# Dense layer in token order inside the attention steps of a fused attention and expert kernel

## Chip, cores and metric

The kernel runs on one core of a Trainium2 chip, as one program in one launch. The metric is the device time of one execution in microseconds (us); the time before is the median of three runs. A further execution was profiled, and every duration below is from that one execution.

## The reference

```python
# attention: 8 batches, 8 heads, 576 tokens, head dimension 64; causal window of 128, ALiBi slopes
scores = scale * np.matmul(q, k.transpose(0, 1, 3, 2))
...
scores = np.where(mask, scores + bias[None], -1000000000.0)
...
attn_out = np.matmul(attn, v)                       # attn: softmax over the keys
x = attn_out.transpose(0, 2, 1, 3).reshape(B * S, H * D)      # 4608 tokens x 512

# feed-forward: one dense pair of layers, and one of 8 expert pairs for each token
h_dense = np.maximum(x @ w1_dense, 0.0)             # 512 x 512
y_dense = h_dense @ w2_dense
logits = x @ w_gate
expert_idx = np.argmax(logits, axis=1)
probs = ...                                         # softmax of the logits
gate_w = probs[np.arange(N), expert_idx]
for e in range(E):
    mask = expert_idx == e
    h = np.maximum(x[mask] @ w1[e], 0.0)
    y_moe[mask] = gate_w[mask, None] * (h @ w2[e])
return y_dense + y_moe
```

## The kernel before

The program has two stages. The first is attention, in 48 steps: 16 units `u` (a batch and half of its heads, four at a time), and three steps `pr` in a unit (query tiles 0 and 1, tiles 2 and 3, and the last 64 rows). For PE, ACT and DVE the order of the instructions is the order of the calls in the loop `for n in range(NS + 9)`; SyncE (SP) and GpSimd (POOL) are ordered by the framework's scheduler, and each runs its own queue in order. In round `n` the loop calls `scores` for step n (a mask product, then q times k, on PE, then the exponentials on ACT, line 373), `norm` for step n-2 (DVE, line 442, which writes the row-major tile `xrow`), `flip` for step n-3 (four PE transposes, then an ACT copy into `xT`, line 470), `attend` for step n-1 (48 small products of 64 or 65 columns, line 426, into the one buffer `ax`), the turning and rounding of the next unit's q and k, and at last `lo` (DVE, line 392), which splits step n's exponentials into two bf16 parts. `scores` has one pair of PSUM tiles (`sq`), `attend` one (`ax`), and everything else shares two PSUM tiles named `misc`.

When a batch is complete, `gate_a` to `gate_d` compute its logits, the expert of each token and the token's row in `xs_dram`, one region of 4608 rows for each expert. Five indirect DMAs on POOL's queue (line 569) then scatter the batch's rows there: 512 values of x in fp32, the gate weight and the token's number. The 18 weight matrices are loaded by POOL's queue meanwhile (line 79), each one held back by a small POOL copy (`tick`, line 588).

After the last batch DVE computes a table of 43 blocks (lines 673 to 749): which expert, which rows. Then the second stage runs 43 blocks of 128 rows. `fetch(j)` gathers a block's rows by an indirect DMA (line 766), four blocks ahead, into one of five buffers. `turn_x` casts and transposes them (lines 777 to 784). `layer1` loads the block's expert number into a PE register (line 801) and multiplies x by the expert's and by the dense weights (lines 814 and 822: four products of 512 columns each, weights moving, x stationary). ACT applies the rectifier twice, with the gate as a scale for the expert's half (lines 830, 831). `turn_h` transposes both halves (line 791), `layer2` multiplies them by both second matrices into one sum (lines 849 and 857), DVE copies it out (line 865), and an indirect DMA scatters the rows to their tokens (line 866). The order in a block is `turn_h(j)`, `layer1(j+1)`, `turn_x(j+2)`, `layer2(j)`, `fetch(j+4)`.

The expert's weights are addressed with the register: `w_all[:, bass.DynSlice(er, 1), 0, kc, :]` stands as the moving operand (`rhs`) in lines 814 and 857. Each such operand has a register operation of PE's sequencer ahead of the instruction that uses it.

Of the kernel before, what the change touches and what calls it, by code (L numbers as in the profile page):

```python
# [23 lines left out]
def kernel(  # L24
# [12 lines left out]
    nc = tc.nc  # L37
# [18 lines left out]

    NB = NTOK // P + E - 1
    NSLOT = (E - 1) * NTOK + NB * P

    RW = DM + 4  # L60
    GC = DM
    TC = DM + 1
# [5 lines left out]

    xs_dram = dram.tile([NSLOT, RW], I32, name="xs_dram")
    w_all = persist.tile([P, E + 1, 2, 4, FF], BF16, name="w_all")  # L70
    basee = persist.tile([P, E], F32, name="basee")

    def load_weights(i):
# [9 lines left out]

    ph1 = ctx.enter_context(ExitStack())
# [4 lines left out]
    ppool = ph1.enter_context(tc.tile_pool(name="ppool", bufs=6))  # L89
    xpool = ph1.enter_context(tc.tile_pool(name="xpool", bufs=2))  # L90
    gs = ph1.enter_context(tc.tile_pool(name="gs", bufs=2))
# [6 lines left out]
    psum_m = ph1.enter_context(  # L98
        tc.tile_pool(name="psum_m", bufs=2, space=bass.MemoryType.PSUM)
    )  # L100

    kTs, vfs = [], []
    for i in range(2):
        kT = abuf.tile([P, 2, SP_], F32R, name=f"kT{i}")
        nc.gpsimd.memset(kT.bitcast(F32)[:, :, S:SP_], 0.0)
        kTs.append(kT)
        vf = abuf.tile([P, NT, 4, D + 1], F32, name=f"vf{i}")
        nc.gpsimd.memset(vf[TAIL:P, NT - 1, :, :], 0.0)
        nc.gpsimd.memset(vf[:, :, :, D : D + 1], 1.0)
        vfs.append(vf)  # L110
    xrows = []
    for i in range(2):
        xrow = abuf.tile([P, NT, RW], F32, name=f"xrow{i}")
        nc.gpsimd.memset(xrow[:, :, TC + 1 : RW], 0.0)
        xrows.append(xrow)
    lt = abuf.tile([P, SP_], F32, name="ltsb")
# [16 lines left out]
    def load_q(u, eng):  # L133
        b, hq = divmod(u, HQ)
        hs = slice(4 * hq, 4 * hq + 4)
        t = ld.tile([P, R, 2, 32], F32, name="qraw", tag="qraw")
# [10 lines left out]
    def load_v(u):  # L147
        b, hq = divmod(u, HQ)
        hs = slice(4 * hq, 4 * hq + 4)
        vf = vfs[u % 2]  # L150
        for i in range(NT):
            rows = min(P, S - i * P)
            nc.sync.dma_start(
                out=vf[:rows, i, :, 0:D],
                in_=v[b, hs, i * P : i * P + rows, :].rearrange("h p d -> p h d"),
            )
# [7 lines left out]
    def round_qk(u, nm):  # L164
        s = tmp.pop((nm, u))
        if nm == "q":
            d = qtp.tile([P, 2, S], F32R, name="qT", tag="qT")
# [9 lines left out]
    def prep_v(u):  # L177
        vf = vfs[u % 2]
# [23 lines left out]
    sc = [ppool.tile([P, 2, 2 * PW], F32, name="p32", tag="p32") for _ in range(2)]  # L202
# [41 lines left out]
    def more_constants():  # L244
# [39 lines left out]
        nc.vector.tensor_copy(out=jf, in_=jf_i)  # L284

# [14 lines left out]
    jf = consts.tile([P, NB], F32, name="jf")  # L300
    ident_x = {}

    def pool_constants():
# [17 lines left out]
        nc.gpsimd.iota(base_i, pattern=[[NTOK, E]], base=0, channel_multiplier=0)  # L321
# [12 lines left out]
    def scores(u, pr):  # L334
# [36 lines left out]
        for i in range(2):  # L371
            p32 = ppool.tile([P, 2, 2 * PW], F32, name="p32", tag="p32")
# [7 lines left out]
            plo = ppool.tile([P, 2, 2 * PW], BF16, name="plo", tag="plo")  # L380
# [22 lines left out]
    def attend(u, pr):  # L403
# [31 lines left out]
        def norm():  # L435
            if hq == 0 and pr == 0:
                cur[("xrow", b)] = xrows[b % 2]
            xrow = cur[("xrow", b)]
            recip = gs.tile([P, 2, 4], F32, name="recip", tag="recip")
            nc.vector.reciprocal(out=recip[:rows, 0:nt], in_=ax_v[:rows, 0:nt, :, D])  # L440
            xo = xrow[:rows, qis[0] : qis[0] + nt, hq * 256 : hq * 256 + 256]
            nc.vector.tensor_tensor(  # L442
                out=xo.rearrange("p t (h d) -> p t h d", h=4),
# [3 lines left out]
            )  # L447

        return norm

    def flip(u, pr):
# [4 lines left out]
        if hq == 0 and pr == 0:  # L456
            cur[("xT", b)] = xpool.tile([P, 4, S], F32, name="xT", tag="xT", bufs=1)
        xT = cur[("xT", b)]
        xrow = cur[("xrow", b)]
        tp = psum_m.tile([P, 2, 2, P], F32, name="tp", tag="misc")  # L460
        for i in range(nt):
            for c in range(2):
                c0 = hq * 256 + c * P
                nc.tensor.transpose(
                    out=tp[:, i, c, 0:rows],
                    in_=xrow[:rows, qis[i], c0 : c0 + P],
# [3 lines left out]
        nc.scalar.copy(  # L470
            out=xT[:, 2 * hq : 2 * hq + 2, q0 : q0 + nt * rows].rearrange(
                "p c (t x) -> p t c x", t=nt
            ),
            in_=tp[:, 0:nt, :, 0:rows],
        )

    scat_group = "scatters"
    gst = {}

    def gate_a(b):  # L480
        xT = cur[("xT", b)]
        HF = S // 2
        for hf in range(2):
            lp = psum_m.tile([P, 512], F32, name="lp", tag="misc")
            for ds in range(4):
                nc.tensor.matmul(  # L486
                    out=lp[32 * ds : 32 * ds + 32, 0:HF],
                    lhsT=wg_pad[:, ds, :],
                    rhs=xT[:, ds, hf * HF : (hf + 1) * HF],
# [3 lines left out]
            nc.scalar.copy(out=lt[:, hf * HF : (hf + 1) * HF], in_=lp[:, 0:HF])  # L493
# [50 lines left out]
    def gate_d(b):  # L544
# [11 lines left out]
        slot = gs.tile([P, NT], I32, name="slot", tag="slot")  # L556
# [10 lines left out]
        for t in range(NT):  # L567
# [6 lines left out]
            )  # L574
            tc.declare_no_dep(
                ins.ins,
                group=scat_group,
                reason="every token has a row of its own",
            )
            tc.add_to_no_dep_group(scat_group, ins.ins)  # L580

    def tick(u, pr, i):
# [3 lines left out]
        xrow = cur[("xrow", u // HQ)]  # L586
        c0 = (u % HQ) * 256
        nc.gpsimd.tensor_copy(  # L588
            out=w_all[:TAIL, e, wi, 0, 0:1], in_=xrow[:TAIL, KP[pr][0], c0 : c0 + 1]
# [3 lines left out]
    NS = len(steps)  # L593
    with tc.manual_schedule(engines={ENG.PE, ENG.Activation, ENG.DVE}):
# [7 lines left out]
        norms, later = {}, {}  # L602
        wnext = 0
        for n in range(NS + 9):
            for f in later.pop(n, []):
# [7 lines left out]
            if 0 <= n - 3 < NS:  # L613
                flip(*steps[n - 3])
                u2, pr2 = steps[n - 3]
                if u2 % HQ == HQ - 1 and pr2 == 2:
                    for i, f in enumerate((gate_a, gate_b, gate_c, gate_d)):
                        later.setdefault(n + 1 + i, []).append(
                            lambda f=f, b=u2 // HQ: f(b)
                        )  # L620
            if n == 0:
                more_constants()
                prep_v(0)
            if 0 <= n - 1 < NS:
                norms[n - 1] = attend(*steps[n - 1])
            if n < NS:
                if pr == 0:
                    if u + 1 < NU:
                        load_v(u + 1)
# [3 lines left out]
                elif pr == 1:  # L633
                    if u + 1 < NU:
                        round_qk(u + 1, "k")
                        turn(u + 1, "q")
                        if u + 2 < NU:
                            load_q(u + 2, nc.sync)
                else:
                    if u + 1 < NU:  # L640
# [4 lines left out]
            if 6 <= n < NS and n % 2 == 0 and wnext < 18:  # L645
                tick(*steps[n - 2], wnext)
                load_weights(wnext)
                wnext += 1
        assert wnext == 18

    ph1.close()

    with ExitStack() as ph2:
        rt = ph2.enter_context(tc.tile_pool(name="route", bufs=1))
        mpool = ph2.enter_context(tc.tile_pool(name="mpool", bufs=3))
        NXR = 5
        xrs = []
        for i in range(NXR):
            xr = rt.tile([P, RW], F32, name=f"xr{i}")
            nc.gpsimd.memset(xr, 0.0)  # L660
            xrs.append(xr)
        psum_t = ph2.enter_context(
            tc.tile_pool(name="psum_t", bufs=1, space=bass.MemoryType.PSUM)
        )
        psum_h = ph2.enter_context(
            tc.tile_pool(name="psum_h", bufs=2, space=bass.MemoryType.PSUM)
        )
        psum_y = ph2.enter_context(
            tc.tile_pool(name="psum_y", bufs=2, space=bass.MemoryType.PSUM)
        )  # L670

        n8 = rt.tile([P, E], F32, name="n8")
        nc.vector.tensor_tensor(out=n8, in0=basee, in1=base0, op=ALU.subtract)
        nb_i = rt.tile([P, E], I32, name="nb_i")
# [245 lines left out]
```

## Time and profile before

| | |
|---|---|
| median of 3 runs | 511.72 us (509.45 to 516.21) |
| profiled execution, device time | 514.72 us |
| its span, first to last instruction | 513.0 us |
| mean granted PE clock | 0.882 |
| busy: PE, DVE, ACT, POOL | 383.8, 304.0, 200.3, 172.5 us |
| last product of `attend` ends | 268.7 us |
| first product of `layer1` starts | 304.1 us |
| last product of `layer2` ends | 503.0 us |

The four last rows cut the span into attention (268.7 us), the wait for the last batch's routing (35.4), the blocks (198.9) and the end (10.0), which add up to 513.0. "PE busy" is a union of modelled instruction spans; a product of 512 columns is shown 379 ns long although the next one starts 216 ns later, so a busy share of PE overstates its load.

### The profile page before, as it was taken

How to read it: one execution, taken by the hardware profiler on the slowest of the kernel's cores; microseconds unless marked ns; L12 is line 12 of the kernel's file. 1: busy time of each engine (PE TensorE's matmuls, PEld its weight loads, DVE VectorE, ACT ScalarE, POOL GpSimd, SP SyncE). 2: the span in 40 equal slices, each digit the busy share in tenths (PEclk: the TensorE clock that was granted, in tenths of full speed). 3: DMA queues.
4: the chain of work that ended last, by engine and by line, in shares of the span. 5: the costliest groups of instructions: out<-in, count | busy, mean ns of one | idle time of the engine just before them, and what ended most of it. 6: DMA issues, size and time to landing. Idle time of an engine off the chain costs nothing.

```text
span 513.0 us, 10730 instructions
## 1 busy us (share of the span) xinstructions
PE 383.8 (75%) x4143; PEld 240.0 (47%) x4180; DVE 304.0 (59%) x567; ACT 200.3 (39%) x287; POOL 172.5 (34%) x244
## 2 busy tenths in 40 slices
PE   1567877778776787777783039899998999889891
PEld 0345555555554556555562015444454444445450
DVE  5879797775977669867471514444444444444441
ACT  2527656626567156671541003323333222322230
POOL 2000016042151321613113433445545455535531
PEclk9999878876799768997696559999999999999997
DMA  4644979879698697986102220323323333323210
GB/s 135 178 115 118 201 156 246 186 187 210 153 251 175 186 209 166 255 159 202 45 24 90 74 82 33 115 91 98 102 86 111 101 124 103 114 83 119 80 52 0
DMA packets 70912, 66.92 MB, mean 130 GB/s; under 512 B 42446, under 2 KB 61902, under 8 KB 70864
## 3 DMA queue, kind: packets, MB, share of 16 engines
q0 software_dynamic: 19328, 37.91, 29.5%
q1 hardware_dynamic: 51140, 28.01, 20.1%
q8 instruction: 34, 0.56, 0.4%
q10 hardware_dynamic: 396, 0.33, 0.2%
q14 instruction: 14, 0.11, 0.1%
HBM read 58.56 MB, written 20.78 MB: 155 GB/s over the span
## 4 chain that ended last, share of the span: by engine, by line
PE 24%; DMA 13%; DVE 5%; issue 3%; ACT 3%; POOL 1%; another core or an unknown queue 1%; POOLq 0%; DVEq 0%
DMA xr<-xs_dram,row_i 13%; PE y L849 4%; PE y L857 4%; PE hd L822 4%; PE hm L814 4%; ACT hr L831 2%; PE hps L791 2%; DVE xm L777 2%; PE xps L780 2%; PE ax L426 1%; PE lp L486 1%; POOL xs_dram L569 1%; PE lg L498 1%; DMA xs_dram<-xrow,slot 1%
## 5 line engine op out<-in xcount | busy, mean ns | idle before, releaser
L426 PE MATMUL ax<-vf,p 128*128 128x65 bf16 (+1 forms) x576 | 74.9, 215 | 50.6 <-DVE xrow L442 44.5
L373 ACT ACTIVATE p<-sq 128x1024 f32<-128x1024 f32 (+1 forms) x96 | 69.3, 776 | 92.5 <-PE sq L363 70.8
L392 DVE TENSOR_TENSOR plo<-p 128x1024 bf16<-128x1024 f32 (+1 forms) x96 | 82.6, 900 | 28.6 <-ACT p L373 23.1
L426 PEld LDWEIGHTS <-p 128*128 128x128 bf16 (+1 forms) x1152 | 69.9, 113 | 61.2 <-DVE xrow L442 51.2
L830 ACT ACTIVATE hr<-hm,xr 128x512 bf16<-128x512 f32 x43 | 29.5, 687 | 159.7 <-PE hm L814 159.7
L426 PE MATMUL ax<-vf,plo 128*128 128x65 bf16 (+1 forms) x576 | 74.3, 212 | 3.9 <-DVE plo L392 2.8
L866 POOL DMA_INDIRECT out_dram<-yo,tok_i x43 | 44.5, 1034 | 97.1 <-DVE hT L797 88.5
L426 PE MATMUL ax<-vl,p 128*128 128x64 bf16 (+1 forms) x576 | 74.4, 211 | 0.3 <-issue 0.3
L569 POOL DMA_INDIRECT xs_dram<-xrow,slot x40 | 42.7, 1067 | 87.2 <-DVE xrow L561 44.9
L426 PEld LDWEIGHTS <-plo 128*128 128x128 bf16 (+1 forms) x576 | 63.1, 113 | 3.4 <-DVE plo L392 3.3
L865 DVE COPY yo<-y 128x512 f32<-128x512 f32 x43 | 29.7, 692 | 58.0 <-PE y L857 54.1
L352 PE MATMUL sq<-mask,ident_b 128*128 128x512 bf16 (+1 forms) x177 | 46.9, 370 | 15.0 <-DVE mask L235 9.2
L766 POOL DMA_INDIRECT xr<-xs_dram,row_i x43 | 43.8, 1019 | 19.9 <-ACT hr L831 11.3
L822 PE MATMUL hd<-w_all,xT 128*128 128x512 bf16 x172 | 45.0, 385 | 0.0
L849 PE MATMUL y<-w_all,hT 128*128 128x512 bf16 x172 | 44.2, 379 | 0.9 <-DVE hT L797 0.9
L780 PE MATMUL xps<-ident_b,xm 128*128 128x128 bf16 x172 | 17.3, 225 | 36.4 <-DVE xm L777 35.8
L857 PE MATMUL y<-w_all,hT 128*128 x172 | 44.1, 379 | 0.0
L814 PE MATMUL hm<-w_all,xT 128*128 x150 | 40.7, 388 | 3.8 <-DMA xr<-xs_dram,row_i 2.7
L363 PE MATMUL sq<-qT,kT 32*128 32x256 f32 (+2 forms) x640 | 34.7, 330 | 3.4 <-ACT qT L168 3.4
L588 POOL CAST w_all<-xrow 64x1 bf16<-64x1 f32 x18 | 8.1, 447 | 85.4 <-DVE xrow L442 85.1
L784 DVE COPY xT<-xps 128x512 bf16<-128x512 bf16 x43 | 18.3, 425 | 31.0 <-PE xps L780 31.0
L363 PEld LDWEIGHTS sq<-qT,kT 32*128 32x128 f32 x640 | 26.3, 217 | 21.9 <-issue 14.4
(115 smaller groups left out, 570.2 us busy)
## 6 DMA issues: line engine op xcount, KB each, us to landing
kraw<-in_k_dram SPq DMA_DIRECT2D x16, 576.0 KB
vf<-in_v_dram SPq DMA_DIRECT2D x64, 128.0 KB
w_all<-in_moe_w_dram POOLq DMA_DIRECT2D x16, 512.0 KB
qraw<-in_q_dram SPq DMA_DIRECT2D x62, 128.0 KB
vf<-in_v_dram SPq DMA_DIRECT2D x16, 64.0 KB
w_all<-in_moe_w_dense_dram POOLq DMA_DIRECT2D x2, 512.0 KB
qraw<-in_q_dram SPq DMA_DIRECT2D x15, 64.0 KB
xr<-xs_dram,row_i POOLq DMA_INDIRECT x43, 3.4
```

The source lines that it names most:

```text
L352: nc.tensor.matmul(out=sq[g // 2][:, g % 2, 0:tot], lhsT=ident_b, rhs=rhs, start=True, stop=False,)
L363: nc.tensor.matmul(out=sq[g // 2][:, g % 2, i * wid : i * wid + nq], lhsT=kT[32 * g : 32 * g + 32, c, kj * P : kj * P + P], rhs=qT[32 * g ...
L373: nc.scalar.activation(out=p32[:, :, 0:tot], in_=sq[i][:, :, 0:tot], func=ACT.Exp, scale=SCALE,)
L392: nc.vector.tensor_tensor(out=plo[:, :, 0:tot], in0=p32[:, :, 0:tot], in1=phi[:, :, 0:tot], op=ALU.subtract,)
L426: nc.tensor.matmul(out=ax[:rows, i, o0 : o0 + w], lhsT=lhs, rhs=rhs, start=(n == 1), stop=(n == 3 * len(kl)),)
L569: ins = nc.gpsimd.indirect_dma_start(out=xs_dram[:, :], out_offset=bass.IndirectOffsetOnAxis(ap=slot[:rows, t : t + 1], axis=0), in_=xrow. ...
L766: nc.gpsimd.indirect_dma_start(out=xm_i.bitcast(I32)[:, :], out_offset=None, in_=xs_dram[:, :], in_offset=bass.IndirectOffsetOnAxis(ap=row ...
L814: nc.tensor.matmul(out=hm, lhsT=xT[:, kc, :], rhs=w_all[:, bass.DynSlice(er, 1), 0, kc, :], start=(kc == 0), stop=(kc == 3),)
L822: nc.tensor.matmul(out=hd, lhsT=xT[:, kc, :], rhs=w_all[:, E, 0, kc, :], start=(kc == 0), stop=(kc == 3),)
L849: nc.tensor.matmul(out=y, lhsT=hT[:, c, :], rhs=w_all[:, E, 1, c, :], start=(c == 0), stop=False,)
L857: nc.tensor.matmul(out=y, lhsT=hT[:, 4 + c, :], rhs=w_all[:, bass.DynSlice(er, 1), 1, c, :], start=False, stop=(c == 3),)
L866: nc.gpsimd.indirect_dma_start(out=out[:, :], out_offset=bass.IndirectOffsetOnAxis(ap=tok_i[:, 0:1], axis=0), in_=yo[:, :], in_offset=None ...
```

## The change

The dense pair of layers leaves the blocks. It is computed in token order, batch by batch, inside the attention steps (`dense1`, `dense2`, from a bf16 copy `xTb` of the transposed x, with eight products of 512 x 288 and five of 128 x 512 a batch), and its fp32 result is scattered by five more indirect DMAs a batch to `ys_dram`, at the same rows as x. x itself is scattered in bf16. A block fetches both rows by two plain DMAs on SP's queue, addressed by a register, does the expert alone, and adds the dense row when it leaves PSUM.

The expert's first layer now has the weights as the stationary operand, so that its result comes out transposed and `turn_h` goes. The first 16 blocks are taken from whole blocks that the first six batches fill, so that their table is computed during attention; the rest are routed after the last batch. Rows behind an expert's last one are filled by 16 DMAs (`fill_x`, `fill_y`) with a token number out of range. The two stages become one loop, and the last batches' gates and dense products run between the first blocks. Three v buffers instead of two; v is loaded a unit earlier; the weights are loaded from the first round on, the first three without a hold.

```diff
@@ norm: x in fp32 for the transposes, and a cast of it into xrow
+            xf = xpool.tile([P, 2, 256], F32, name="xf", tag="xf")
-            xo = xrow[:rows, qis[0] : qis[0] + nt, hq * 256 : hq * 256 + 256]
...
+            nc.vector.tensor_copy(
+                out=xrow[:rows, qis[0] : qis[0] + nt, hq * 256 : hq * 256 + 256],
+                in_=xf[:rows, 0:nt],
+            )
@@ flip: two copies out of PSUM instead of one
+        for dst in (cur["xT"], cur[("xTb", b)][:, 2 * hq : 2 * hq + 2, :]):
+            nc.scalar.copy(
+                out=dst[:, :, q0 : q0 + nt * rows].rearrange(
...
@@ gate_a: for each unit, on half the rows of lt, instead of for each batch
@@ new
+    def dense1(b, c, hf):
...
+        hp = psum_m.tile([P, 512], F32, name="hp", tag="misc")
+        for kc in range(4):
+            nc.tensor.matmul(
+                out=hp[:, 0:HF],
+                lhsT=w_all[:, E, 0, kc, c * P : c * P + P],
+                rhs=xTb[:, kc, hf * HF : hf * HF + HF],
+                start=(kc == 0),
+                stop=(kc == 3),
+            )
+        nc.scalar.activation(
+            out=hT[:, c, hf * HF : hf * HF + HF], in_=hp[:, 0:HF], func=ACT.Relu
+        )
+
+    def dense2(b, t):
...
+        yp = psum_m.tile([P, 512], F32, name="yp", tag="misc")
+        for c in range(4):
+            nc.tensor.matmul(
+                out=yp[:rows, :],
+                lhsT=hT[:, c, t * P : t * P + rows],
+                rhs=w_all[:, E, 1, c, :],
...
+        yt = xpool.tile([P, DM], F32, name="yt", tag="yt")
+        nc.scalar.copy(out=yt[:rows, :], in_=yp[:rows, :])
+        ins = nc.gpsimd.indirect_dma_start(
+            out=ys_dram[:, :],
...
+    def dense_items(b):
+        one = [lambda c=c, h=h: dense1(b, c, h) for h in range(2) for c in range(4)]
+        two = [lambda t=t: dense2(b, t) for t in range(NT)]
+        return [one[0:2], one[2:4], one[4:6], one[6:8], two[0:2], two[2:5]]
@@ routing in two tables
+    def route_late():
...
+        for e in range(E):
+            r = nc.values_load(
+                base_r[0:1, e : e + 1],
+                engines=[ENG.SP],
...
+            ins = nc.sync.dma_start(
+                out=xs_dram[bass.DynSlice(r, P), :], in_=fill_x.bitcast(I32)[:, :]
+            )
...
@@ a block
+    def fetch(j):
+        r = nc.values_load(where[j][1], engines=[ENG.SP], ...
+        xr = mpool.tile([P, RW], F32, name="xr", tag="xr", bufs=4)
+        yr = mpool.tile([P, DM], F32, name="yr", tag="yr", bufs=4)
+        for nm, t, src in (("x", xr, xs_dram), ("y", yr, ys_dram)):
+            ins = nc.sync.dma_start(
+                out=t.bitcast(I32)[:, :], in_=src[bass.DynSlice(r, P), :]
+            )
...
     def layer1(j):
...
+        hp = psum_h.tile([P, 4, P], F32, name="hpm", tag="hpm")
+        for c in range(4):
+            for kc in range(4):
+                nc.tensor.matmul(
+                    out=hp[:, c, :],
+                    lhsT=w_all[:, bass.DynSlice(er, 1), 0, kc, c * P : c * P + P],
+                    rhs=xT[:, kc, :],
+                    start=(kc == 0),
+                    stop=(kc == 3),
+                )
+        hT = mpool.tile([P, 4, P], BF16, name="hTm", tag="hTm")
+        nc.scalar.activation(out=hT, in_=hp, func=ACT.Relu)
...
     def layer2(j):
...
+                rhs=w_all[:, bass.DynSlice(er, 1), 1, c, :],
...
+        nc.vector.scalar_tensor_tensor(
+            out=yo,
+            in0=y,
+            scalar=xr[:, GC : GC + 1],
+            in1=yr,
+            op0=ALU.mult,
+            op1=ALU.add,
+        )
+        ins = nc.gpsimd.indirect_dma_start(
+            out=out[:, :],
...
+    AHEAD = 3
+
+    def block(j):
...
+        if j + 1 < NB:
+            layer1(j + 1)
+        if j + 2 < NB:
+            turn_x(j + 2)
+        layer2(j)
+        if j + AHEAD + 1 < NB:
+            fetch(j + AHEAD + 1)
@@ the loop
+        while jm < NB:
...
+            todo = items.pop(n, [])
+            for f in todo[:1]:
+                f()
             if 0 <= n - 1 < NS:
                 norms[n - 1] = attend(*steps[n - 1])
+            for f in todo[1:]:
+                f()
...
+            while wnext < 2 * (E + 1) and n < NS and wnext <= 2 + 16 * (n - 3) / 42:
+                if n > 4:
+                    pace(wnext)
                 load_weights(wnext)
                 wnext += 1
+            if n == NS + 1:
+                ph1.close()
...
+                for j in range(AHEAD + 1):
+                    fetch(j)
+            if n > NS + 1:
+                block(jm)
+                jm += 1
```

Seen in the program that results: each of `layer1`'s 16 products has a register operation ahead of its weight load and another ahead of the product itself, 32 in a block, and `layer2`'s four products have one each; before, a block had eight in all. The scatter of block j, which reads the token numbers in `xr`, has to land before `fetch(j+4)` may write that buffer. ACT's third copy into `yt` in a batch waits for the first scatter out of `yt` to land, the fourth for the second, the fifth for the third.

## The prediction

> **What bounds the kernel now.** I read the busy shares by stage first, because the mean over the span mixes stages. Columns: PE, PEld, DVE, ACT, POOL busy (instructions), granted clock, DMA share, GB/s.
>
> ```profile
> 60.00:260.00 200.00, 155.11 (x2297) 112.14 (x2303) 148.07 (x250) 110.46 (x155) 57.00 (x68) 0.81 0.78 183
> 268.70:304.00 35.30, 5.73 (x42) 3.95 (x44) 11.12 (x42) 1.69 (x5) 14.95 (x20) 0.55 0.28 91
> 304.00:503.00 199.00, 182.87 (x1178) 94.80 (x1198) 90.62 (x168) 55.22 (x86) 91.30 (x122) 0.99 0.29 91
> ```
>
> In attention no engine is full: of 200 us PE works 155 and DVE 148, at a granted clock of 0.81. The 35.3 us behind it hold little but scatters and tables. In the blocks PE works 183 of 199 us at full clock. The list of waits between 60 and 260 us says what attention's engines wait for (total, times, longest).
>
> ```profile
> PEld L426 <- DVE xrow L442: 38.2, 24, 5.6
> PE ax L426 <- DVE xrow L442: 33.0, 18, 5.5
> DVE plo L392 <- ACT p L373: 20.9, 10, 4.3
> DVE vl L181 <- DMA vf<-in_v_dram: 9.4, 6, 2.5
> DVE qs L161 <- DMA qraw<-in_q_dram: 6.8, 3, 3.2
> ```
>
> It is a ring: `attend` waits for DVE to empty `ax`, DVE for ACT's exponentials, ACT for PE's scores. Units start 16.1 us apart (exponentials of step pr=0 at 62.73 in u3, 256.49 in u15); PE idles 3.5 of these, DVE works 11.9, ACT 8.9.
>
> For the blocks I took the chain that ended last, one stretch of it (start, length, what).
>
> ```profile
> 393.34 3.37 DMA xr<-xs_dram,row_i
> ...
> 397.70 0.86 PE y L849 x4
> 398.56 0.86 PE y L857 x4
> 399.43 0.45 PE hps L791 x8
> 399.88 0.86 PE hm L814 x4
> 400.74 0.88 PE hd L822 x4
> 401.62 0.02 issue
> 401.64 0.61 ACT hr L831
> 402.25 0.19 issue
> 402.44 3.33 DMA xr<-xs_dram,row_i
> ```
>
> A block is 3.9 us of PE work, and a loop through the fetch closes over two blocks: 402.44 − 393.34 = 9.1, or 4.55 each; 43 blocks take 198.9, or 4.63 each. PE's array and the transfer loop stand side by side, so relieving one alone brings little. The last view is PE's sequencer, which reads registers (ns min/median/max; first and last start).
>
> ```profile
> L857 PEldq FUSED_REGOPS  x172: 55/55/55, 310.2 to 501.5; - x172
> L801 PEldq TENSOR_LOAD <-er_i x43: 297/328/570, 303.0 to 494.6; - x43
> ```
>
> A register operation lasts 55 ns, but consecutive ones start 133 apart (median of 258 gaps between the four of a layer). So register operation, weight load with a fixed address and product with a register address together occupy the sequencer 133 ns. Fixed pairs go at up to 31 ns each (`attend`: 48 pairs in 1.5 us). A product with a register address therefore costs between 133−55−31 = 47 and 133−55 = 78 ns of sequencer time. I take 62, between them. In before this is hidden: eight in a block are 1.1 us of 4.6.
>
> **The change, part by part**, against the profiled execution (span 513.0 = attention 268.7 + gap 35.4 + blocks 198.9 + end 10.0; 1.7 more outside it).
>
> *Gap.* Sixteen blocks are routed from six batches, so the first blocks need no last gate. Between the last `attend` and the first block remain the scores' tail, PSUM changing hands, a fetch (landings 2.0 to 3.4) and a transpose: 4 us instead of 35.4, bounds 2 and 10. The second table (`route_late`, DVE, near block 7) and the last batch's ten scatters move in between the blocks. The first table, 7.3 us of DVE (the old one ran 288.0 to 295.9) and 2.2 more, moves into steps 43 and 44; DVE is in attention's ring, so I count 4.
>
> *Block, sequencer.* `layer1` issues 16 weight loads and 16 products, all addressed by the register: 32 register operations, where before had four there. A pair costs 2 × (55 + 62) = 234 ns; with 47 and 78 it is 204 and 266; if a load with a register address were as cheap as a fixed one, 188. Sum: register load to first register operation 0.51 (0.40 to 0.67 in before) + 16 × 0.234 = 3.74 + `layer2` 4 × 0.133 = 0.53 + four transposes 0.12 = 4.90 us. Bounds 4.06 (by 188), 4.3 and 5.5.
>
> *Block, the rest.* Array work shrinks to 16 × 0.056 + 0.86 + 0.22 = 2.0 us, hidden under the sequencer. DVE does 0.43 + 0.69, ACT 0.6, POOL one indirect DMA of 1.0: all beside. Gone are the dense half and `turn_h`, 2.2 us of PE's array. The transfer loop: `fetch(j+4)` waits for the scatter of block j; `layer2` 1.05, `yo` 0.69, 0.8 to the issue, scatter 2.1, two DMAs on SP 2.0 to 3.4, 0.3 to the cast: 7.1 to 8.3 over two blocks, 3.55 to 4.2 each. The fetch leaves POOL's queue (1.0 us of POOL each) for SP's, where only the next fetches, and once the fills, stand behind its wait; who waits for them is `turn_x` on DVE two blocks later. The loop stays under 4.9; if the sequencer were quick, this would be the floor. So 43 × 4.90 = 210.7 instead of 198.9.
>
> *Extras among the blocks.* SP's queue holds 16 fills (395 KB a pair, 3.2 MB; attention's `kraw`, 576 KB, lands in 3.8 us) between fetch(10) and fetch(11). POOL issues ten scatters about 1.3 us apart ahead of some blocks' `out`. With four blocks fetched ahead most is hidden: 5 + 4 = 9, bounds 0 and 25 (3.2 MB at `kraw`'s rate is 21, plus 4).
>
> *Attention.* A unit gets half a batch's dense work. PE: 16 × 0.121 (288 of 512 columns, 0.215 at full length) + 10 × 0.215 = 4.1 us at full clock. ACT: a second copy of `flip` 1.47, four rectifiers 1.6, 2.5 copies of `yt` 1.5, in all 5.0 with half a gate copy. DVE: the cast into `xrow`, 1.1. ACT goes from 8.9 to 13.9, DVE from 11.9 to 13.0, both below 16.1. On PE, 12.5 + 4.1 = 16.6 at most, 14.3 if the longer busy stretches bring the clock to 1.00. The cover is PE's idle time behind `xrow`, 3.5 a unit at most; the ring's order is fixed, the dense products stand ahead of and behind `attend`, and both `misc` tiles are shared, so I let two thirds (2.4) fit and charge 1.7 × 16 = 27. With full cover it is 0, without any 4.1 × 16 = 66. Also, ACT's third, fourth and fifth `yt` copies wait for scatters of 5.3 us; behind them ACT has `qT` and the next exponentials, and PE's scores wait for those. Against it, v is loaded a unit earlier and the 9.4 us of waits for it may go, the bound below nothing. With 4 for the table, attention's surplus is 31, bounds −9 and 70. Three unheld weight loads at the start: 0 to 4, taken 0.
>
> *Sum.* 268.7 + 31 + 4 + 210.7 + 9 + 10 = 533.4 span, 535.1 device time, 20.4 above its 514.7. Against the median, 3.0 lower: 532.
>
> **A rule against the row.** The trace's row is the 133 ns spacing, which is longer than a product of 128 columns takes in the array (56). The Trainium skill, "TensorE: Matmul & The Clock Gate", section "Back-to-back issue gap", gives about 81 ns for each sustained pair of weight load and 128-column matmul, as a rule of array and weight loads alone. By it `layer1` would be an estimated 16 × 0.081 = 1.3 us, the block would fall to its transfer loop of 4.2, and the sum to about 502. The same page, "Step-by-step: what each phase is for", puts a matmul decoded in microcode at about 62 ns, which speaks for the sequencer as a bound. The row decides; attention's 31 ns pairs already differ from the 81.
>
> **Rivals.**
> - *The sequencer keeps up* (faster). Loads with a register address overlap more than products do, as the 31 ns pairs suggest, and the block falls to 3.7, inside the transfer loop's 3.55 to 4.2: 43 × 1.2 = 52 less, 480. Against it: nothing in before shows such a load. It decides below 4.19 us a block, where the whole is 2% under the median.
> - *Attention swallows the dense work* (within 2%). PE's idle 3.5 a unit takes all of it and the clock rises; the surplus is the table's 4: 532 − 27 = 505. For it: a first unit undisturbed took 11.7 us. Against it: two `misc` tiles and a fixed order.
> - *The yt and xf buffers stall the ring* (slower, above the forecast). Scatters of 5.3 us behind two `yt` tiles hold ACT, and the single qT tile makes that PE's wait: all 4.1 us show, surplus 70, 571. It decides once ACT's wait passes PE's idle 3.5 a unit.
> - *The early start fails* (slower). If the first fetch waits for all scatters, not those of six batches, the gap stays near 25 instead of 4: 553. The diff's manual dependencies name six batches, which speaks against it.
>
> **How the numbers follow.** Forecast 0.50, its own range 512 to 552 (attention's surplus 15 to 45, block 4.7 to 5.1); sequencer 0.16; swallowed 0.20; stall 0.09; no early start 0.05. The likeliest is 532. For 8 in 10 the range goes from 500, which takes in most of the 505 case and leaves out the 480 one, to 562, short of the 571 case. About 2%, 501.5 to 522, is what a measurement of this kernel can tell from no change. Faster has the sequencer case and the low edge of the swallowed one, 0.17; within 2% the rest of that and the forecast's low end, 0.21; slower the remainder, 0.62.
>
> **What would show it.** In the changed profile: PE sequencer gaps of about 117 ns between register operations in `layer1` and blocks 4.9 apart (wrong if 4.2 or less); units of some 17.8 us with waits of ACT for `ys_dram` and of PE for `misc`; first block within 10 us of the last `attend`; no pause over 10 us near block 10. A surplus of attention under 10 us, or blocks under 4.2, makes the forecast wrong; both in full would give 532 − 27 − 52 = 453.

## The result, and the profile after

The changed kernel takes 668.71 us (median of four runs, 665.05 to 672.0). Before takes 513.97 beside it; the ratio is 1.302 (95% interval 1.289 to 1.316). The forecast was 532 with a range of 500 to 562: the direction is right, the size is not, 20 us forecast and 155 measured.

The same cut of the span, in us (the profiled executions):

| | before | forecast | after |
|---|---|---|---|
| attention, to the last product of `attend` | 268.7 | 268.7 + 31 | 416.9 |
| gap to the first product of `layer1` | 35.4 | 4 | 10.4 |
| 43 blocks | 198.9 | 210.7 + 9 | 232.5 |
| end | 10.0 | 10 | 9.5 |

The busy shares by stage, with the columns of the first view before:

```profile
60.00:260.00 200.00, 145.99 (x1706) 95.22 (x1720) 110.19 (x194) 101.48 (x175) 47.56 (x56) 0.80 0.52 130
416.90:427.20 10.30, 6.65 (x33) 3.16 (x34) 1.30 (x4) 4.12 (x9) 2.90 (x3) 0.99 0.68 209
506.00:659.70 153.70, 146.85 (x761) 74.20 (x771) 38.37 (x65) 19.11 (x32) 31.27 (x32) 0.83 0.41 127
```

In the 200 us in the middle of attention every engine does less than before, ACT included: 101 us instead of 110, although each unit gives it more to do. So the ring is slower because its members wait longer, not because one of them is full. The waits in the same stretch (total, times, longest):

```profile
ACT yt L666 <- DMA ys_dram<-yt,slot: 21.7, 9, 4.7
ACT hTd L649 <- remote: 20.0, 3, 7.1
DVE recip L462 <- remote: 15.0, 2, 7.5
PEld lp L513 <- ACT yt L666: 14.8, 6, 4.7
```

Units are now 26.0 us apart (exponentials of step pr=0 at 110.1 in u4, 370.2 in u14) instead of 16.0 (78.0 and 238.0). A batch, two units, shows two holes. The first, on the chain that ended last (start, length, what): ACT may not write the third `yt` before the scatter of the first has landed, then the same with the next, and PE's `lp` stands behind ACT.

```profile
222.11 6.37 DMA ys_dram<-yt,slot
...
228.57 0.59 ACT yt L666
...
229.43 3.79 DMA ys_dram<-yt,slot
...
233.32 0.59 ACT yt L666
233.91 0.04 issue
233.95 1.18 PE lp L513 x4
```

The second hole comes with the five scatters of x. In the window DVE has 0 instructions and ACT 0.01 us in 7 us; in the timeline (start, length, engine, line, what, idle time before) ACT waits 7.07 us for PE's products of `dense1`, which PE's own rows show over at 205.1. It goes on at 209.08, after POOL has issued its fifth scatter at 206.97:

```profile
202.00:209.00 7.00, 3.96 (x48) 2.61 (x45) 0.00 (x0) 0.01 (x1) 4.66 (x5) 0.74 0.59 176
```

```profile
203.15 0.97 POOL L599 DMA_INDIRECT xs_dram<-xrow,slot  x1 [0.30 <-issue]
204.00 1.15 PE L642 MATMUL hp<-xTb,w_all 128*128 128x288 bf16 x4
...
206.97 0.91 POOL L599 DMA_INDIRECT xs_dram<-xrow,slot  x1 [0.30 <-issue]
209.02 0.21 DVE L462 RECIPROCAL recip<-ax 128x8 f32<-128x8 f32 x1 [7.46 <-remote]
209.08 0.41 ACT L649 ACTIVATE hTd<-hp 128x288 bf16<-128x288 f32 x1 [7.07 <-remote]
```

"Remote" means that the profile found no releaser. Engines tell each other of finished work by semaphores, and the trace has the times of these signals. Set against PE's modelled ends, most of PE's signals arrive within 0.02 us, but here they come late, the one above by 3.9 us (205.15 to 209.08), and there is a like group in each batch. I call these late completions.

In the blocks the sequencer sets the pace, as forecast: 1376 register operations, 32 a block, and each pair in `layer1` starts 0.23 us after the one before (median 227 ns between products). A steady block takes 4.76 us.

```profile
L881 PEldq FUSED_REGOPS  x1376: 3/55/724, 426.0 to 657.5; - x197
```

```profile
440.18 0.22 PE hpm L881
440.41 0.22 PE hpm L881
440.64 0.22 PE hpm L881
```

### The profile page after: what moved, and what is told of

Its sections match the earlier page's. It is cut to its first block, busy times and chain, and to the rows that moved or that the text cites. A ratio compares the mean times of both kernels' runs of the same rounds, so it can differ in the third digit from the quotient of the medians.

```text
span 669.2 us, 12798 instructions
## 1 busy us (share of the span) xinstructions
PE 492.8 (74%) x4378; PEld 287.9 (43%) x4424; DVE 286.2 (43%) x567; ACT 241.3 (36%) x412; POOL 148.2 (22%) x193
## 4 chain that ended last, share of the span: by engine, by line
issue 32%; PE 20%; DMA 18%; ACT 8%; POOL 8%; DVE 7%; another core or an unknown queue 3%; SPq 2%; POOLq 1%; ACTq 0%; DVEq 0%
DMA ys_dram<-yt,slot 11%; POOL out_dram L913 5%; PE hpm L881 4%; DMA qraw<-in_q_dram 4%; PE sq L373 3%; ACT p L394 3%; POOL xs_dram L599 3%; PE hp L642 3%; DVE plo L413 2%; PE sq L384 2%; PE lp L513 2%; DMA vf<-in_v_dram 2%; PE y L897 1%; ACT yt L666 1%
## 5 line engine op out<-in xcount | busy, mean ns | idle before, releaser
L881 PE MATMUL hpm<-xTm,w_all 128*128 128x128 bf16 x688 | 137.2, 240 | 12.0 <-DVE xTm L866 4.2
L881 PEld LDWEIGHTS <-w_all 128*128 x688 | 68.9, 106 | 91.9 <-issue 33.3
L913 POOL DMA_INDIRECT out_dram<-yo,xr x43 | 42.1, 979 | 173.8 <-DVE yo L905 159.0
L642 PE MATMUL hp<-xTb,w_all 128*128 128x288 bf16 x256 | 48.1, 317 | 34.1 <-ACT xTb L497 32.6
L667 POOL DMA_INDIRECT ys_dram<-yt,slot x40 | 41.6, 1040 | 112.1 <-ACT yt L666 107.4
L513 PE MATMUL lp<-xT,wg_pad 128*32 128x288 f32 x128 | 31.0, 585 | 45.4 <-ACT yt L666 21.8
L447 PEld LDWEIGHTS <-plo 128*128 128x128 bf16 (+1 forms) x576 | 61.9, 111 | 4.4 <-DVE plo L413 4.4
L897 PE MATMUL y<-w_all,hTm 128*128 x154 | 58.2, 502 | 1.9 <-issue 1.1
L658 PE MATMUL yp<-w_all,hTd 128*128 128x512 bf16 (+1 forms) x147 | 43.6, 408 | 19.6 <-ACT yt L666 13.1
L649 ACT ACTIVATE hTd<-hp 128x288 bf16<-128x288 f32 x64 | 27.2, 425 | 72.0 <-remote 44.9
L905 DVE SCALAR_TENSOR_TENSOR yo<-y,xr,yr 128x512 f32<-128x512 f32 x43 | 32.3, 750 | 38.5 <-PE y L897 36.0
```

The source lines that it names most:

```text
L447: nc.tensor.matmul(out=ax[:rows, i, o0 : o0 + w], lhsT=lhs, rhs=rhs, start=(n == 1), stop=(n == 3 * len(kl)),)
L513: nc.tensor.matmul(out=lp[r0 : r0 + 32, 0:HF], lhsT=wg_pad[:, 2 * (u % HQ) + c, :], rhs=cur["xT"][:, c, hf * HF : (hf + 1) * HF], start=Tr ...
L642: nc.tensor.matmul(out=hp[:, 0:HF], lhsT=w_all[:, E, 0, kc, c * P : c * P + P], rhs=xTb[:, kc, hf * HF : hf * HF + HF], start=(kc == 0), s ...
L658: nc.tensor.matmul(out=yp[:rows, :], lhsT=hT[:, c, t * P : t * P + rows], rhs=w_all[:, E, 1, c, :], start=(c == 0), stop=(c == 3),)
L667: ins = nc.gpsimd.indirect_dma_start(out=ys_dram[:, :], out_offset=bass.IndirectOffsetOnAxis(ap=slots[b][:rows, t : t + 1], axis=0), in_=y ...
L881: nc.tensor.matmul(out=hp[:, c, :], lhsT=w_all[:, bass.DynSlice(er, 1), 0, kc, c * P : c * P + P], rhs=xT[:, kc, :], start=(kc == 0), stop ...
```

## The experiments

All times in us. The times of after and of e7 to e10 are medians of several executions, the others are one execution each; the first columns cut the profiled span as above. The groups of runs stood on different chips: before, run beside them, took 516.2 (e1 to e4), 513.8 (e5 to e8), 505.6 (e9 to e12), 518.5 (e13 to e15) and 518.8 (e16 to e18). And two executions differ: e6's attention is 8.1 shorter than after's, though its edit lies in the blocks alone. Differences of attention of a few us are therefore not read as effects below.

| run | attention | gap | blocks | end | time |
|---|---|---|---|---|---|
| after | 416.9 | 10.4 | 232.5 | 9.5 | 668.7 |
| e1 dense2 in three steps | 388.6 | 6.5 | 231.2 | 9.5 | 637.6 |
| e2 scatters of x in five steps | 383.2 | 10.8 | 235.0 | 9.3 | 640.1 |
| e3 both | 357.4 | 5.7 | 232.1 | 9.7 | 606.7 |
| e4 no dense work | 293.6 | 5.6 | 218.3 | 6.1 | 525.4 |
| e5 as e3, scatters in three steps | 362.0 | 5.8 | 232.3 | 9.6 | 611.5 |
| e6 fixed expert | 408.8 | 10.4 | 187.5 | 9.5 | 618.2 |
| e7 before, scatters in three steps | 269.0 | 35.1 | 197.6 | 10.1 | 514.7 |
| e8 dense in the blocks, early routing | 292.5 | 5.9 | 184.2 | 6.1 | 489.4 |
| e9 as e8, q loaded once | 281.4 | 4.1 | 179.3 | 6.1 | 471.1 |
| e10 as e9, weights held | 275.2 | 4.0 | 179.3 | 6.1 | 465.6 |
| e11 as e3, quarter of the products | 355.2 | 4.6 | 229.5 | 9.7 | 600.8 |
| e12 as e3, q once, weights held | 341.5 | 5.7 | 229.1 | 9.3 | 587.3 |
| e13 as e3, flip first | 356.8 | 5.7 | 231.2 | 9.7 | 605.2 |
| e14 as e3, dense copies on DVE | 428.3 | 9.4 | 234.6 | 9.3 | 683.3 |
| e15 as e12, flip first | 345.0 | 5.7 | 234.7 | 9.3 | 596.5 |
| e16 as e13, quarter of the products | 355.5 | 4.9 | 231.7 | 9.7 | 603.6 |
| e17 as e3, no scatter of y | 338.7 | 5.7 | 229.4 | 6.1 | 581.6 |
| e18 as e16, no scatter of y | 332.1 | 4.7 | 228.0 | 6.5 | 572.9 |

**The two holes.**

```diff
@@ e1: dense_items, by step
-        return [one[0:2], one[2:4], one[4:6], one[6:8], two[0:2], two[2:5]]
+        return [[], one[0:3], one[3:6], one[6:8], two[0:2], two[2:3], two[3:5]]
@@ e2: gate_d issues the first scatter of x, each later step one more
+        scatter_x(b, xrow, 0)
+        for t in range(1, NT):
+            gates.setdefault(gst["n"] + t, []).append(
+                lambda b=b, xrow=xrow, t=t: scatter_x(b, xrow, t)
+            )
...
+        nc.vector.tensor_copy(out=sc_t, in_=slots[b][:, t : t + 1])
```

> The five second-layer items of a batch stand in three steps (2, 1, 2) instead of two (2, 3), and the first layer in steps two to four, so that the scatter out of each yt buffer has a step of its own to land before ACT writes that buffer again. Theory yt (ACT's wait for its two yt buffers, 45 us between 100 and 400 us, sets attention's surplus): attention 45 us shorter, 625 us in all. Theory burst (PE's completions arrive 3 to 5 us late while POOL issues five scatters of x back to back, and ACT and DVE stand still for 7 us a batch): within 10 us of 669. Theory work (the ring has no room for 8 us of PE and 10 us of ACT a batch): within 10 us of 669, the wait only changes its name.

> The five scatters of x of a batch are issued one in each of five steps (each behind a small copy of its slot column on DVE) instead of back to back. Theory burst: the 7 us in which ACT and DVE stand still in each batch go to 1 or 2, 40 us less, 630 us. Theory yt and theory work: within 10 us of 669.

> Both spreads together. If both causes are real and separate: 85 us less, 585 us. If the work itself sets the surplus: still over 640 us.

Attention falls by 28.3 (e1), 33.6 (e2) and 59.4 (e3): both holes are real, and they nearly add (61.9). 45 and 40 were expected, and e3's time lies between its two cases. In e1 ACT's wait for landings of y falls from 45.1 to 16.4 within attention, so that what went off the list is what was gained; its edit also regroups the first layer's items. In e2 the "remote" waits of ACT and DVE are gone, and a new wait has come, of DVE's cast into `xrow` for the scatters that are now spread out (38.8). What ACT now waits for is PE's products as such, 1.1 us at a time:

```profile
ACT hTd L657 <- PE hp L650: 21.3, 20, 3.2
```

Late completions of over 1 us stand in five groups between 60 and 360 us in after, one to a batch (around 105, 158, 208, 259 and 313 us); in e2 no such group is left. So the burst of scatters makes the groups. What in the chip delays the signal is not shown.

**Without dense work, and the row tile.**

```diff
@@ e4: fetch_in no longer fetches yr, the last copy of a block adds none, and the loop
-                    for i, fs in enumerate(dense_items(b2)):
-                        items.setdefault(n + 1 + i, []).extend(fs)
@@ e5: as e3, two scatters in the first step, and
-            gates.setdefault(gst["n"] + t, [])
+            gates.setdefault(gst["n"] + t // 2, [])
```

> The dense products, their scatters and the fetches of the dense rows are left out (the output lacks the dense half); the blocks and the early routing stay. All theories: attention near that of before, 275 to 290 us, and 530 to 545 us in all. What it tells: if the 7 us stand-still of each x burst is still there without dense items, the burst alone makes it (attention nearer 300); if it is gone, it needs a dense item behind it.

> As the kernel with both spreads, but the five scatters of x stand in three steps (2, 2, 1) instead of five, so that the last has landed before the row tile is written for the next batch but one; there DVE's cast into it waited 47 us between 100 and 350 us for these scatters. Theory late rows: attention 15 to 25 us shorter than 357, 580 to 592 us in all. Theory work (what is left of attention's surplus over the kernel without dense items, 64 us, is PE's and ACT's work on them): within 8 us of 607.

e4 puts dense work at 416.9 − 293.6 = 123.3 us of attention, and 14 us of the blocks. Its units are 16.1 us apart, as in before, with the bursts back to back, and "remote" waits of ACT and DVE come to 2.2 us between 60 and 420 (67.4 in after): without a dense item in the ring the bursts cost nothing that shows. Its attention still ends 24.9 later than in before, and 20.9 of this stand at the start (u4 begins at 98.9 instead of 78.0). In e5 DVE's wait for late rows, 46.8 us in e3, is gone, but attention is not shorter: ACT's wait for landings of y grows from 13.1 to 19.7 between 100 and 350 us, and DVE's for ACT's exponentials from 24.5 to 51.2. Taken away alone, the late rows are worth nothing.

**The block's sequencer.**

```diff
@@ e6: layer1 and layer2
-                    lhsT=w_all[:, bass.DynSlice(er, 1), 0, kc, c * P : c * P + P],
+                    lhsT=w_all[:, 0, 0, kc, c * P : c * P + P],
...
-                rhs=w_all[:, bass.DynSlice(er, 1), 1, c, :],
+                rhs=w_all[:, 0, 1, c, :],
```

> The changed kernel with expert 0's weights at fixed addresses in both layers of a block: no register operations, everything else the same (the output is that of expert 0 for all rows). Theory sequencer (32 register operations of 113 ns make the block's 4.76 us): blocks fall to the transfer loop, 3.6 to 4.2 us, 620 to 645 us in all. Rival (the transfer loop or a chain over ACT and DVE already sets the block): 4.6 us or more, over 660 us.

The steady block falls from 4.76 to 4.08 (24 blocks between the `out` scatters at 503.2 and 601.0), and the stage by 45.0. In equal stretches PE's busy time, which was full, drops to 60%; the first line is after, the second e6:

```profile
550.00:600.00 50.00, 47.85 (x248) 24.46 (x251) 12.23 (x21) 5.97 (x10) 10.75 (x11) 0.80 0.41 126
```

```profile
550.00:600.00 50.00, 29.58 (x297) 20.58 (x294) 14.44 (x26) 7.45 (x13) 11.74 (x12) 0.93 0.50 156
```

That is the sequencer. At 4.08 the transfer loop (3.55 to 4.2 in the prediction) takes over: between 503 and 600 us PE's first transposes of a block wait 41.1 us for landings of `xr`, where they waited 5.2 in after. The total, 618.2, lies just under its forecast of 620 to 645; attention, which the edit doesn't touch, was 8.1 shorter.

**Before, and the early routing alone.** e7 gives before the scatters of e5. e8 computes the dense layers in the blocks again, as before does, with x stationary and the weights moving in the expert's first product, rows fetched five blocks ahead, and keeps the routing from six batches; no `yr` is written or fetched.

```diff
@@ e8: layer1, first the expert's product, then the dense one; turn_h then transposes hr
+                lhsT=xT[:, kc, :],
+                rhs=w_all[:, bass.DynSlice(er, 1), 0, kc, :],
...
+                    lhsT=w_all[:, E, 0, kc, c * P : c * P + P],
+                    rhs=xT[:, kc, :],
@@ e9
-        load_q(2, nc.sync)
@@ e10
-            while wnext < 2 * (E + 1) and n < NS and wnext <= 2 + 16 * (n - 3) / 42:
+            if 6 <= n < NS and n % 2 == 0 and wnext < 2 * (E + 1):
```

> The kernel before, with its five scatters of x in three steps (2, 2, 1). Theory burst: the late completions of PE seen there (2 to 3.5 us around 109, 175 and 239 us) go, 5 to 12 us less, 500 to 508 us. Rival (in before they are hidden by other work): within 4 us of 512.

> The changed kernel's early routing, bf16 rows and one loop, but the dense pair in the blocks again (first layer with fixed weights stationary, 16 products of 128 columns), the expert's first layer with weights moving as before (8 register operations a block), scatters of x in three steps, fetches five blocks ahead. Theory: the loss is the dense work inside attention's ring plus the late completions, and the early routing is worth its 25 us. Attention 270 to 280, gap 6, blocks 43 x 4.2 to 4.4 and 8 more, end 10: 475 to 495 us, faster than both. Rival (the early tables and the bf16 rows cost attention what the gap gives): attention 290 or more, 505 us or more.

> The kernel with the dense pair in the blocks and early routing (e8), without the second issue of the loads of q for unit 2 ahead of the loop, which the loop issues again. In e8 units 1 and 2 start 10 and 20 us later than in before. Theory double load (q's one buffer is filled twice, and the second filling waits for the first to be used): unit 2 starts 8 to 10 us earlier, 479 to 482 us. Rival (all 20 us come from the three weight loads and the early v that fill the queues): within 3 us of 489.

> e9 with the weight loads from round 6 on, every second round, each held, as in before; the first three no longer go out at the start. Theory weights: they share the queues with the first q, k and v (q of unit 1 took 7 us to land), another 4 to 9 us less, 471 to 477 us. Rival (q of unit 1 is late because eight loads of v stand ahead of it on SP's queue): within 3 us of e9.

e7: ratio 1.004 (0.9995 to 1.008). In before the late completions are hidden. e8: ratio 0.957 (0.951 to 0.962), within its forecast in total; its attention stays at 292.5, where 270 to 280 was expected and the rival had 290 or more, and the early gap is worth 29.5. The late start is seen on after's chain: three landings of q, of 6.5 to 7.2 us, stand one behind the other, and the last two are the same data, since q of unit 2 is issued ahead of the loop and again in it, into one buffer.

```profile
28.57 7.07 DMA qraw<-in_q_dram
...
39.75 6.54 DMA qraw<-in_q_dram
...
48.73 7.15 DMA qraw<-in_q_dram
```

e9 has 11.1 us less of attention than e8 (ratio 0.934, 0.928 to 0.939), e10 6.2 less again (ratio 0.923, 0.917 to 0.929). Both times lie under their forecasts, since before is 1.6% faster on their chip; on the chip of e8 the ratios would give 480 and 474, as forecast. The start itself shows what each edit is worth: the first exponentials of unit 2 stand at 68.2 in e8, 60.6 in e9 and 53.9 in e10 (48.3 in before). So the double load and the unheld weights are two terms of the late start, 7.6 and 6.7, or 14.3 together. e10 is faster than both kernels. Its blocks are full on PE at full clock, with a steady block of 3.93 us:

```profile
279.20:458.50 179.30, 172.99 (x1538) 110.91 (x1567) 68.24 (x169) 56.07 (x89) 46.18 (x47) 0.98 0.29 94
```

**The 64 us that are left between e3 and e4.**

```diff
@@ e11, e16, e18: one product in each group of dense1 and dense2
-        for kc in range(4):
+        for kc in range(1):
@@ e13, e15, e16, e18: the loop calls flip ahead of scores
+            if 0 <= n - 3 < NS:
+                flip(*steps[n - 3])
             lo = None
@@ e17, e18: dense2 writes no y, and no block fetches or adds yr
-        ins = nc.gpsimd.indirect_dma_start(
-            out=ys_dram[:, :],
@@ e14
-        nc.scalar.copy(out=yt[:rows, :], in_=yp[:rows, :])
+        nc.vector.tensor_copy(out=yt[:rows, :], in_=yp[:rows, :])
```

> The kernel with both spreads (e3), but each dense product group makes one product instead of four (the dense half then holds a quarter of its sums); copies, buffers, scatters and their order stay. Theory PE time (what is left of the dense surplus, 64 us, is 4.1 us of PE a unit without cover): three quarters of 66, some 45 to 55 us less, 552 to 562 us. Rival (the hand-over between PE and ACT through the two shared misc tiles and ACT's own time): at most 20 us less, 587 us or more.

> The kernel with both spreads (e3), with q of unit 2 loaded once and the weights held as in e10. If the late start is a term of its own: 15 to 20 us less than 607, 587 to 592 us. Were the dense work in attention cheap once the stalls are out, it would come near 520; every theory here says that it stays over 570.

> e3 (both spreads) with each round's flip ahead of its scores instead of behind them. In e3 the second dense item of a step waits for the misc tile of the flip, which ACT empties only behind the exponentials of the scores (1.94 us, then two copies of 0.6); with the flip first, ACT empties it while PE does the scores. Theory hand-over (this wait, 0.8 to 1.5 us a step in some 40 steps, is most of the 64 us that are left of the dense surplus): 30 to 55 us less, 552 to 577 us. Theory ACT time (5 us more of ACT a unit fill the ring): within 8 us of 607.

> e3 with the rectifier of the dense first layer and the copy into yt on DVE instead of ACT (3.1 us a unit leave ACT, for DVE, which is busy 62% there). Theory ACT time: 30 to 50 us less, 557 to 577 us. Theory hand-over (the flip's tile still waits behind ACT's exponentials): at most 12 us less, 595 us or more; if DVE, whose split of the exponentials is in the ring too, becomes the later one, more than 607.

> e13 with q of unit 2 loaded once and the weights held. The gains of e12 and e13 add: 20 us less than e13. The dense work in attention would then cost (its attention against 275 us without it in e10) what PE and ACT can't hide.

> e13 (both spreads, flip ahead of the scores) with one product instead of four in each dense group (a quarter of the dense sums). Alone, neither edit shortened attention by over 2 us. Theory two limits (PE's own stream and the hand-over behind ACT's exponentials stand side by side, so that taking away one bares the other): both together give 30 us or more, at most 575 us. Theory elsewhere (a wait that neither touches, the scatters' above all): 595 us or more.

> e3 without the five scatters of y in a batch and without the blocks' fetch of the dense rows (the dense products and their copies remain, their result is dropped). In e3 ACT still waits 13 us for landings between 100 and 350 us, and PE 14 us for ACT behind it. Theory elsewhere: attention 20 to 35 us less than 357. Theory two limits: at most 15 us less.

> e16 without the scatters of y and the fetch of the dense rows. If the three causes (PE time, hand-over, scatters of y) make up the 64 us, attention comes within 15 us of the 294 of the kernel without dense items; if it stays over 325, ACT's own time on the dense copies is the rest.

Three quarters of PE's dense products are worth 2.2 us of attention (e11, on the fastest chip), the flip ahead of the scores 0.6 (e13), both together 1.9 (e16): no more than executions differ by. But one wait stands in all of these runs, since they keep e3's scatters of x: DVE's cast into `xrow` waits for them to land. Between 100 and 360 us it is 46.8 us in e3, and it grows to 66.0 in e11, 57.8 in e13 and 59.2 in e16. What the edits save may have gone into this wait, so they show only that PE's time and the flip's hand-over gain nothing while it stands. e5, which takes the wait away and leaves the work, gains nothing either; two limits side by side would look like this, and no run took away this wait and part of the dense work together, short of e4, which leaves out all of the dense work.

Work moved from ACT to DVE costs 70.9 (e14), as the last case of its expectation had it; by which wait is not shown. Without the scatters of y attention is 18.7 shorter (e17, between its two theories; the edit takes away their traffic and issue too, not ACT's wait alone), and in e18, with both other edits as well, 25.3. Mending the start works in e12 (unit 2 begins 15.0 earlier, attention is 15.9 shorter); with the flip first unit 2 begins 14.6 earlier, attention is 11.8 shorter and the time 8.7, where 20 was expected (e15).

So 38.5 us are left between e18 and e4 (attention 332.1 and 293.6), and what they are is not settled. By its expectation e18, at over 325, speaks for ACT's own time on the dense copies. The mean over units seems to agree: ACT works 2.8 us a unit more than in e4, and units are 3.1 longer. But e18's units are not alike. From u6 to u13 short ones (15.0 to 15.9 us) and long ones (22.1 to 24.3) take turns. The lines are u8 and u9:

```profile
178.10:193.10 15.00, 11.37 (x184) 7.70 (x183) 10.93 (x19) 12.59 (x21) 3.96 (x5) 1.00 0.68 175
193.10:215.30 22.20, 15.58 (x203) 10.50 (x202) 15.98 (x33) 13.82 (x26) 3.40 (x5) 0.85 0.59 121
```

In the short unit ACT does 12.6 us of work, three copies of `yt` among it, against 10.4 to 10.6 in e4's units, and the unit is no longer than those (14.4 to 17.6). The long one has only 1.2 us more of ACT's work, and it holds the wait for the scatters of x: 6.2 us there, and none in the short ones. Between 100 and 300 us this wait comes to nearly all of the 38.5; e4 has none of it.

```profile
DVE xrow L469 <- DMA xs_dram<-xrow,sct: 36.8, 10, 7.2
```

So these rows speak for the landing of x in the long units rather than for ACT's time in series. It is argued, not shown: the run that would decide, e18 with e5's scatters, was not made.

## Why the prediction was wrong, and where it was right

**The step that failed** is attention's: "I let two thirds (2.4) fit and charge 1.7 × 16 = 27", with "without any 4.1 × 16 = 66" as its upper end. The dense work cost 123.3 (e4). The step priced PE's array time against PE's idle time and put two waits at nothing that have little to do with either. ACT's wait for `yt` was named, but had a price only as a rival's condition: 28.3 by e1. The late completions behind the bursts of scatters were not in the sum at all: 33.6 by e2. Together they are 59.4 (e3). Late completions were there in before too, hidden (e7), and could be seen: the list of waits between 60 and 260 us, from which the prediction shows five lines, also has this one, larger than two of the five, and I passed over it.

```profile
ACT p L373 <- remote: 14.2, 3, 5.1
```

A stall of 6 us in an ordered ring should have been summed by itself, batch by batch, not inside the fraction that PE's idle time covers. What is left without the two holes, 63.8 us between e3 and e4, lies just under the 66 of no cover at all, but this is no proof of that price: 18.7 of it go with the scatters of y (e17), and the cause of the rest stays open.

**The start** was "0 to 4, taken 0". e9 and e10 measure 14.3 at unit 2, 6.7 for the weights and 7.6 for the second load of q. The prediction counted the weights alone; the second load, which the change's code has, was missing from the sum.

**The extras** among the blocks were 9; they are 232.5 − 43 × 4.76 = 27.8. In e4 they are 13.6, somewhat more than was said for the fills and the late table, and 14 go with the dense items of the last batches and the fetch of their rows, which the step had put into attention's sixteen units.

**The gap** was 4 and is 10.4, just outside its bounds (2 to 10). It follows the place of the dense items: 6.5 with e1's order of them, 5.6 without them (e4).

**The block** was right in mechanism and size: 4.90 forecast, 4.76 measured. A register operation and its weight load or product take 113 ns (forecast 117, from a loading of 47 to 78 ns on a 55 ns operation), and the floor under it was forecast at 3.55 to 4.2 and is 4.08. The rule set against the row, "TensorE: Matmul & The Clock Gate", section "Back-to-back issue gap" of the Trainium skill, gives 81 ns for a pair at 128 columns: here a pair takes 227 ns with register addresses, and 56 with fixed ones (e6, e8, e10), so it holds for neither, and the measurements decide. The 62 ns that "Step-by-step: what each phase is for" on that page gives for a matmul decoded in microcode are near what is left of the 113 after the register operation, 58; no run here shows how these instructions are decoded.

**The rivals.** The quick sequencer and the swallowed dense work did not happen. The early start worked. The stall of `yt` was the nearest at 571, given 0.09, and was priced at PE's 66 too; its mechanism explains 28 of 123 us by e1, and 47 at most, if all that e17 gains is counted to it.

The range ended at 562 because the upper bound of the largest term was PE's time. Worked out afterwards from this case's rows, what an item adds on every engine that it passes, 4.1 on PE, 5.0 on ACT and 1.1 on DVE a unit, makes 163 us. That would have bounded the measured 123, but it holds none of the waits that e1 and e2 measured, so that it is no test of the account.

Two small sums of the prediction are off without weight: the transfer loop's lower end adds up to 6.9 over two blocks, not 7.1, and attention's lower bound of −9 leaves out the 4 for the table.

## What to carry to other kernels

Where a few engines hand work round in a written order, price every buffer that waits for a DMA landing by the landing, and look in the profile before the change for waits without a releaser; the idle share of the busiest engine is no price for these. And when a wait is taken away and nothing is gained, look whether another one has grown by as much (e11, e5). A gain that is separate from the rest of a change (here the early routing, whose gap fell from 35.4 to 5.9 in e8) is worth taking out and running alone: with the dense layers left in the blocks and the start mended it gave a kernel of 0.923 of the time. Count register operations before making weights with a register address stationary: 32 in a block made it take 4.76 us, where 4.08 would do without them (e6).

## What the runs showed of the hardware that was not expected

While POOL issues five indirect DMAs back to back, some 1.27 us apart, PE's signals to other engines arrive up to some 4 us after the modelled end of its products, several in a row (after, 208 us); issued one in a step, no such group is left (e2). No signal of DVE or ACT in after is over 1 us late. Pairs of weight load and 128-column product run at 56 ns with fixed addresses (e6, e8, e10) and at 227 ns with register addresses (after).
